# A planned attention kernel: first batch by head pairs, first weights ahead of later loads, second-batch masks by DMA

## The chip, the cores and the metric

The kernel runs on one core of a Trainium2 chip. The metric is device time in microseconds. Five instruction streams matter here, TensorE (PE in the profile), VectorE (DVE), ScalarE (ACT), GpSimd (POOL) and SyncE (SP), which issues most DMAs, and beside them the DMA queues. In the traces below each engine works through its own stream in order: an instruction that waits holds up what stands behind it on that engine.

The kernel before takes 283.2 us (median of 3, 282.56 to 283.69).

## The reference, cut to what matters

```python
# q, k, v: (4, 8, 768, 64) fp32; w_in: (512, 2048); w_out: (2048, 512)
gate = q @ mean_of_each_64_keys(k).T            # 12 key blocks; blocks after the query's own: -1e9
sel  = top3(gate) | {own block}                 # per query and head
attn = softmax(where(sel and causal, q @ k.T / 8, -1e9)) @ v
x    = attn.transpose(0, 2, 1, 3).reshape(3072, 512)
out  = gelu_tanh(x @ w_in) @ w_out              # (3072, 512) fp32
```

A batch is 768 rows and eight heads, which the kernel treats as four head pairs. Pairs 0 to 3 are batch 0, pairs 4 to 7 batch 1, and so on. For each batch the kernel runs attention, then the first linear layer with its gelu ("s1", 16 tiles of 1.30 us of TensorE), then the second ("s2").

## The kernel before

The kernel is a list of operations with estimated costs, dependencies and priorities. A planner inside the kernel, run while the kernel is built, walks a clock forward, picks an engine and a start time for every operation, and then emits all operations in the order of these planned starts. So the planner's estimates do not cost time themselves: they fix the order in which each engine must take its instructions. What an instruction really waits for at run time is its data, through semaphores.

```python
def load(p, key, at_least):                       # k, q or v of head pair p
    ...
    go = add({SP: 0.2}, emit_t if dve else emit,  # SyncE issues it: planned 0.2 us
             [free_sd.get((key, p - ...))], prio=10 * p)
    ld[key, p] = add({"DMA": 4.5 if dve else 2.0}, lambda _: None, [go, at_least],
                     prio=1000 * b + hp)          # planned: 4.5 us of DMA for a k or q from pair 5 on

def pre(p):                                       # preparation of one head pair
    ...                                           # k, q turned; block sums ks; ksb = masked sums
    for c in range(1, NC):                        # gate scores: five matmuls, 24 columns each
        nc.tensor.matmul(plan.buf["gt", p][:, (c - 1) * 24:c * 24],
                         T["qT32", p][:, c * 128:(c + 1) * 128], T["ksb", p]..., ...)
    ...                                           # top 3 of each row -> madd (DVE)
    if by_xbar(p):                                # pairs 8 to 15: mask turned by a DMA transpose
        go = add({SP: 0.1}, mask_dma, [sel], pr)
        m = add({"XBAR": 2.5}, lambda _: None, [go], pr)
    else:                                         # pairs 0 to 7: mask turned by TensorE
        m = add({PE: 0.27}, mask, [sel], pr, takes=("pre", ("mk", p)))
    mcs = [add({DVE: 0.4, ACT: 0.6}, mc(h), [m, ...], pr) for h in range(2)]   # mask copies

def heads(p):                                     # one head at a time: scores, exp, select, PV
    ...                                           # K = 76 rows: 64 of k/q and 12 of mask
```

SyncE issues the loads, by the trace, as k, q, v of pairs 0, 1 and 2, then k3 q3 k4 q4 v3 k5 q5; w_in starts at 29.6 us, beside q of pair 5, so the first loads of batch 1 go ahead of it. w_out is triggered from GpSimd when v3 and three attention outputs of batch 0 are planned to be there.

The softmax here doesn't subtract the row's maximum and nothing guards it: scores larger than these inputs give would overflow.

Of the kernel before, what the change touches and what calls it, by code (L numbers as in the profile page):

```python
# [33 lines left out]
class Plan:  # L34
# [17 lines left out]
    def solve(self):  # L52
        for n, op in enumerate(self.ops):
            op.n = n
            op.left = len(op.deps)
            op.ready = 0.0
            op.users = []
        for op in self.ops:
            for d in op.deps:
                d.users.append(op)  # L60
# [10 lines left out]
        while cand:  # L71
            best = None
            ests = []
            for op in cand:
# [13 lines left out]
                key=lambda x: (x[3].prio, x[3].n, x[1]))  # L88
# [32 lines left out]
def kernel(  # L121
# [22 lines left out]
    FIRST_DVE = 5  # L144
# [8 lines left out]
    atp = ctx.enter_context(tc.tile_pool(name="atp", bufs=7))  # L153
# [12 lines left out]
    bmask = const.tile([128, 2, NBLK], FP32)  # L166
# [5 lines left out]
    w_out16 = persist.tile([128, NF, DM], FP16)  # L172
    qT16, kT16, v16, madd = [], [], [], []
# [16 lines left out]
    def copy(eng, out, in_):  # L190
        if eng == ACT:
            nc.scalar.copy(out=out, in_=in_)
        else:
            nc.vector.tensor_copy(out=out, in_=in_)

    def by_dve(p):
        return p >= FIRST_DVE

    def by_xbar(p):
        return p >= 2 * HP  # L200
# [3 lines left out]
    ld = {}  # L204
    free_sd = {}

    def load(p, key, at_least):
# [11 lines left out]
        def emit_t(_):  # L219

            sd = io.tile([128, NC * 4, 32], FP32, tag=key, name=f"{key}_sd_{p}")
            for hh in range(2):
                for a in range(2):
# [5 lines left out]
        dve = key != "v" and by_dve(p)  # L229
        go = add({SP: 0.2}, emit_t if dve else emit,  # L230
                 [free_sd.get((key, p - (PV if key == "v" else PF)))],
                 prio=10 * p)
        ld[key, p] = add({"DMA": 4.5 if dve else 2.0}, lambda _: None, [go, at_least],
                         prio=1000 * b + hp)

    def cast_v(p, old):
        b, hp = divmod(p, HP)

        def emit(eng):
            copy(eng, v16[p % NB][:, :, :, 0:64], T["v", p])  # L240
        free_sd["v", p] = ld["v16", p] = add(
            {DVE: 0.47, ACT: 0.8}, emit, [ld["v", p], old],
            prio=1000 * (b - 1) + 599 + hp if b else 100 * hp - 55)

    def load_w(name, dst, src, n, deps, prio):
        res = []
        view = src.rearrange("(i p) f -> p i f", p=128)

        def emit(_):
            nc.gpsimd.dma_start(out=dst, in_=view)  # L250
        go = add({POOL: 1.3}, emit, deps, prio=prio)
        return add({"DMA": 12.0}, lambda _: None, [go], prio=prio)


    c_E = {}

    def consts():
        def e16(_):
            E32 = hd2.tile([128, S], FP32, tag="kT32", name="E32")
            T["E16"] = E16 = E32[0:12].bitcast(FP16)[:, 0:S]  # L260
            nc.gpsimd.memset(E16, MASKVAL)
            nc.gpsimd.affine_select(
                out=E16.rearrange("p (n w) -> p n w", w=64),
                in_=E16.rearrange("p (n w) -> p n w", w=64),
                compare_op=ALU.is_equal, fill=0.0,
                base=0, pattern=[[1, NBLK], [0, 64]], channel_multiplier=-1)
        c_E["E"] = add({POOL: 2.0}, e16, [], prio=-50)

        def gates(_):

            T["cgate"] = cgate = const.tile([128, NG, NBLK], FP32, name="cgate")
# [16 lines left out]

        def fill(i):
            def emit(_):  # L290
                for h in range(2):
                    nc.vector.tensor_copy(out=kT16[i][h][64:76, :],
                                          in_=T["E16"])
                    nc.vector.memset(qT16[i][h][64:76, 0:128], 0.0)
            c_E["fill", i] = add({DVE: 0.8}, emit, [c_E["E"]],
                                 prio=100 * i - 30)
# [4 lines left out]
            c_E["ones", i] = add({POOL: 0.5}, emit_p, [], prio=-40 + i)  # L301
# [7 lines left out]
    def pre(p):  # L309
        b, hp = divmod(p, HP)  # L310
        i = p % NB
        pr = 1000 * (b - 1) + 590 + hp if b else 100 * hp - 60
        slow = 1.0
        old = last.get(p - NB, {})

        def wk_t(a):
            def emit(_):
                w = plan.buf["wk", p, a]
                for c in range(3):
                    nc.tensor.transpose(  # L320
                        w[:, c * 128:(c + 1) * 128],
                        T["k", p][:, 3 * a + c].rearrange("p h d -> p (h d)"),
                        ident32)
            return emit

        def ks_r(a):
            def emit(_):
                if a == 0:
                    T["ks", p] = hd.tile([128, NBLK], FP32, tag="ks",
                                         name=f"ks_{p}")  # L330
                nc.vector.tensor_reduce(
                    out=T["ks", p][:, 6 * a:6 * a + 6],
                    in_=plan.buf["wk", p, a][:, 0:HALF].rearrange(
                        "p (n w) -> p n w", w=64),
                    op=ALU.add, axis=AXL.X)
            return emit

        def kc(a, h):
            def emit(eng):
                copy(eng, kT16[i][h][0:64, a * HALF:(a + 1) * HALF],  # L340
                     plan.buf["wk", p, a][64 * h:64 * h + 64, 0:HALF])
            return emit

        kcs, ksr, qcs = [], [], []
# [10 lines left out]
        if by_dve(p):  # L355
            t = add({DVE: 0.83}, tr("k"),
# [3 lines left out]
            def ks_all(_):  # L360
                T["ks", p] = hd.tile([128, NBLK], FP32, tag="ks",
                                     name=f"ks_{p}")
                nc.vector.tensor_reduce(
                    out=T["ks", p],
                    in_=T["kT32", p].rearrange("p (n w) -> p n w", w=64),
                    op=ALU.add, axis=AXL.X)
            ksr.append(add({DVE: 0.83}, ks_all, [t], pr))
# [6 lines left out]
            kcs = [add({DVE: 0.47, ACT: 0.7}, kc_all(h),  # L374
                       [t, old.get("k", None)], pr + 0.1) for h in range(2)]
        for a in range(0 if by_dve(p) else 2):
            t = add({PE: 0.33 * slow}, wk_t(a),
                    [ld["k", p], last.get(p - 3, {}).get("pre")], pr,
                    takes=("pre", ("wk", p, a)))
            if a == 1:  # L380
                free_sd["k", p] = t
            r = add({DVE: 0.47}, ks_r(a), [t] + ksr, pr)
            ksr.append(r)
            c0 = add({DVE: 0.47, ACT: 0.38}, kc(a, 0),
                     [t, old.get("k", None)], pr)
            c1 = add({DVE: 0.47, ACT: 0.38}, kc(a, 1),
                     [t, old.get("k", None)], pr)
            kcs += [c0, c1]
            add({"NONE": 0.0}, lambda _: None, [r, c0, c1], pr,
                gives=[("wk", p, a)])  # L390

        def ksb_m(_):
            T["ksb", p] = hd.tile([128, 2, NBLK], FP32, tag="ksb",
                                  name=f"ksb_{p}")
            nc.vector.tensor_tensor(
                out=T["ksb", p], in0=bmask,
                in1=T["ks", p].unsqueeze(1).to_broadcast([128, 2, NBLK]),
                op=ALU.mult)
        ksb = add({DVE: 0.1}, ksb_m, ksr, pr)
# [4 lines left out]
        def wq_t(a):  # L404
            def emit(_):
                w = plan.buf["wq", p, a]
                for c in range(3):
                    nc.tensor.transpose(
                        w[:, c * 128:(c + 1) * 128],
                        T["q", p][:, 3 * a + c].rearrange("p h d -> p (h d)"),  # L410
                        ident32)
            return emit

        def qc(a):
            def emit(eng):
                if a == 0:
                    T["qT32", p] = hd.tile([128, S], FP32, tag="qT32",
                                           name=f"qT32_{p}")
                copy(eng, T["qT32", p][:, a * HALF:(a + 1) * HALF],
                     plan.buf["wq", p, a][:, 0:HALF])  # L420
            return emit

        if by_dve(p):
            t = add({DVE: 0.83}, tr("q"),
# [3 lines left out]
        for a in range(0 if by_dve(p) else 2):  # L428
            t = add({PE: 0.33 * slow}, wq_t(a), [ld["q", p]], pr,
                    takes=("pre", ("wq", p, a)))  # L430
            if a == 1:
                free_sd["q", p] = t
            qcs.append(add({DVE: 0.47, ACT: 0.5}, qc(a),
                           [t] + qcs + [last.get(p - 3, {}).get("pre")], pr,
                           gives=[("wq", p, a)]))



        g = None
        for c in range(1, NC):  # L440
            def gate(_, c=c):
                nc.tensor.matmul(  # L442
                    plan.buf["gt", p][:, (c - 1) * 24:c * 24],
                    T["qT32", p][:, c * 128:(c + 1) * 128],
                    T["ksb", p].rearrange("p h n -> p (h n)"),
                    start=True, stop=True)
            g = add({PE: 0.1}, gate, [ksb, g] + qcs, pr,
                    takes=("pre", ("gt", p)), lag=0.2)

        def gm_e(_):  # L450
            T["gm", p] = hd.tile([128, NG, NBLK], FP32, tag="gm",
                                 name=f"gm_{p}")
            nc.vector.tensor_tensor(
                out=T["gm", p],
                in0=plan.buf["gt", p][:, 0:NG * NBLK].rearrange(
                    "p (g n) -> p g n", n=NBLK),
                in1=T["cgate"], op=ALU.add)
        gm = add({DVE: 0.2}, gm_e, [g, c_E["gates"]], pr, gives=[("gt", p)])

        def sel_e(_):  # L460
            mx8 = hd.tile([128, NG, 8], FP32, tag="mx8", name=f"mx8_{p}")
            for x in range(NG):
                nc.vector.max(out=mx8[:, x, :], in_=T["gm", p][:, x, :])
            sel = hd.tile([128, NG, NBLK], FP32, tag="sel", name=f"sel_{p}")
# [337 lines left out]
```

## Time and profile before

Lines of the page: the busy time of each engine; the span in 40 slices of 7.03 us, in tenths, for TensorE and for its granted clock; the shares of the chain that ended last.

```profile
PE 266.5 (95%) x2230; PEld 166.9 (59%) x2230; DVE 137.4 (49%) x438; ACT 189.4 (67%) x251; POOL 49.1 (17%) x119
...
PE   5998998799999999998999999999999999999994
...
PEclk9999999999999999999999999999999999999999
...
PE 76%; ACT 15%; DVE 3%; issue 3%; DMA 2%; POOL 1%; ACTq 0%; POOLq 0%; SPq 0%; DVEq 0%
```

TensorE is busy nearly everywhere, its granted clock is full in every slice, and the chain that ended last is 76% TensorE. But the first 50 us are only formally busy: 110 filler matmuls, whose results nobody reads, stand there. The chain of waits in order of time shows what really bounds the start (start us, length us, what):

```profile
49.38 0.93 ACT at_1_1_922 L571
50.37 0.43 POOL at_1_1_922 L585
50.85 0.39 PE bank_92 L597 x7
...
55.21 0.82 ACT gT_1010 L683
...
57.53 0.49 DVE qT_0_107 L194
58.04 0.68 ACT qT_1_108 L192
58.75 0.82 ACT gT_1010 L683
59.61 1.46 PE wide_88 L670 x8
```

Exponentials on ACT up to 51 us, then the first gelu at 55.21, then, after two waits of 0.5 us, s1 of batch 0 in steps of 1.30 us without a pause. (57.53 and 58.04 are the two copies of the mask of pair 4.)

| stage (us) | before |
|---|---|
| last exponential of batch 0 ends | 51.1 |
| first gelu of batch 0 | 55.2 |
| s1 of batches 0, 1, 2, 3 ends | 75.4, 140.6, 201.5, 256.8 |
| end of the span | 281.2 |

### The profile page before, as it was taken

What the parts mean: (1) busy time and instruction counts of PE and PEld (TensorE: products, weight loads), DVE (VectorE), ACT (ScalarE), POOL (GpSimd) and SP (SyncE); (2) the same over time, 40 slices, a digit from 0 to 9 for tenths busy, and PEclk for the clock granted to TensorE, in tenths of its full rate; (3) what the DMA queues carried; (4) which work ended last, traced back from release to release, by engine and by line L of the source; (5) the groups of instructions that cost most, each with busy time, mean ns of one, the idle gap of its engine ahead of it and who ended that gap; (6) DMA issues with size and microseconds to landing.
All of it is one profiled execution on the core that took longest, in us unless ns stands there. A gap on an engine that the chain in (4) does not pass through costs nothing.

```text
span 281.2 us, 5780 instructions
## 1 busy us (share of the span) xinstructions
PE 266.5 (95%) x2230; PEld 166.9 (59%) x2230; DVE 137.4 (49%) x438; ACT 189.4 (67%) x251; POOL 49.1 (17%) x119
## 2 busy tenths in 40 slices
PE   5998998799999999998999999999999999999994
PEld 4777775555657566564667565666566645565441
DVE  4587955770088787755578885594114310000000
ACT  2568998765889759476599992487799923664111
POOL 8012524100024213000024430000034400000000
PEclk9999999999999999999999999999999999999999
DMA  8999999999999987997667242230112231000212
GB/s 169 217 220 207 138 212 148 177 197 167 131 166 166 207 161 143 204 163 109 114 130 151 70 121 84 81 48 2 23 40 70 54 105 75 0 0 2 75 75 75
DMA packets 129211, 33.01 MB, mean 117 GB/s; under 512 B 123552, under 2 KB 125600, under 8 KB 129184
## 3 DMA queue, kind: packets, MB, share of 16 engines
q1 hardware_dynamic: 126592, 28.46, 54.2%
q0 software_dynamic: 2592, 4.19, 8.6%
q8 instruction: 17, 0.28, 0.4%
q14 instruction: 10, 0.08, 0.1%
HBM read 27.26 MB, written 6.29 MB: 119 GB/s over the span
## 4 chain that ended last, share of the span: by engine, by line
PE 76%; ACT 15%; DVE 3%; issue 3%; DMA 2%; POOL 1%; ACTq 0%; POOLq 0%; SPq 0%; DVEq 0%
PE wide_88 L670 13%; PE wide_89 L670 13%; PE bank_90 L700 9%; PE bank_93 L700 7%; PE bank_91 L700 6%; PE bank_92 L700 5%; PE wide_88 L559 4%; PE wide_89 L559 4%; DMA mT_1959<-madd_118 2%; PE bank_93 L597 1%; PE bank_92 L442 1%; PE bank_90 L734 1%; PE bank_91 L442 1%; PE bank_92 L597 1%; PE bank_91 L734 1%
## 5 line engine op out<-in xcount | busy, mean ns | idle before, releaser
L670 PEld LDWEIGHTS <-w_in_105 128*128 128x128 f16 x512 | 50.3, 103 | 32.3 <-issue 3.4
L700 PEld LDWEIGHTS <-gT_3361 128*128 128x128 f16 x96 | 9.4, 98 | 11.2
L734 PEld LDWEIGHTS <-ident_99 128*128 128x128 f16 x110 | 11.8, 115 | 5.6 <-DVE ident_99 L165 3.0
L700 PEld LDWEIGHTS <-gT_2670 128*128 128x128 f16 x96 | 9.0, 98 | 7.9
L670 PE MATMUL wide_89<-xT_1398,w_in_105 128*128 128x512 f16 x64 | 12.4, 325 | 1.4 <-ACT gT_1836 L683 1.4
L700 PEld LDWEIGHTS <-gT_1836 128*128 128x128 f16 x96 | 9.1, 99 | 7.7
L670 PE MATMUL wide_88<-xT_546,w_in_105 128*128 128x512 f16 x64 | 12.2, 325 | 1.1 <-ACT gT_1010 L683 1.1
L700 PEld LDWEIGHTS <-gT_1010 128*128 128x128 f16 x96 | 9.3, 104 | 6.1
L700 PE MATMUL bank_90<-w_out_106,gT_1836 128*128 128x512 f16 x48 | 12.7, 379 | 0.0
L670 PE MATMUL wide_88<-xT_2289,w_in_105 128*128 128x512 f16 x64 | 12.6, 325 | 0.0
L670 PE MATMUL wide_88<-xT_1398,w_in_105 128*128 128x512 f16 x64 | 12.6, 325 | 0.0
L670 PE MATMUL wide_89<-xT_2289,w_in_105 128*128 128x512 f16 x64 | 12.2, 325 | 0.0
L670 PE MATMUL wide_89<-xT_546,w_in_105 128*128 128x512 f16 x64 | 12.2, 326 | 0.0
L670 PE MATMUL wide_88<-xT_3039,w_in_105 128*128 128x512 f16 x64 | 12.0, 326 | 0.0
L670 PE MATMUL wide_89<-xT_3039,w_in_105 128*128 128x512 f16 x64 | 11.7, 326 | 0.0
L734 PE MATMUL bank_90<-ident_99 128*128 128x256 f16 x27 | 7.8, 303 | 3.5 <-DVE ident_99 L165 3.0
L530 ACT ACT_TABLE_LOAD x8 | 10.3, 1283 | 0.9 <-PEq L786 0.8
L734 PE MATMUL bank_92<-ident_99 128*128 128x256 f16 x38 | 9.8, 292 | 0.0
L700 PE MATMUL bank_93<-w_out_106,gT_1010 128*128 128x512 f16 x32 | 9.7, 379 | 0.0
L683 ACT ACTIVATE gT_1010<-wide_88 128x768 f16<-128x768 f32 x8 | 6.5, 809 | 4.2 <-PE wide_88 L670 4.2
L683 ACT ACTIVATE gT_2670<-wide_88 128x768 f16<-128x768 f32 x8 | 6.5, 807 | 4.2 <-PE wide_88 L670 4.2
L700 PE MATMUL bank_91<-w_out_106,gT_2670 128*128 128x512 f16 x32 | 9.2, 379 | 0.0
(917 smaller groups left out, 673.9 us busy)
## 6 DMA issues: line engine op xcount, KB each, us to landing
w_in_105<-in_moe_w_in_dram POOLq DMA_DIRECT2D x1, 2048.0 KB, 13.6
w_out_106<-in_moe_w_out_dram POOLq DMA_DIRECT2D x1, 2048.0 KB, 17.7
k_sd_136<-in_k_dram SPq DMA_DIRECT2D x2, 192.0 KB, 3.0
q_sd_143<-in_q_dram SPq DMA_DIRECT2D x2, 192.0 KB, 4.0
v_sd_148<-in_v_dram SPq DMA_DIRECT2D x2, 192.0 KB, 4.4
k_sd_153<-in_k_dram SPq DMA_DIRECT2D x2, 192.0 KB, 4.5
q_sd_158<-in_q_dram SPq DMA_DIRECT2D x2, 192.0 KB, 4.6
v_sd_163<-in_v_dram SPq DMA_DIRECT2D x2, 192.0 KB, 4.4
```

Of the source, the lines that this page charges most:

```text
L442: nc.tensor.matmul(plan.buf["gt", p][:, (c - 1) * 24:c * 24], T["qT32", p][:, c * 128:(c + 1) * 128], T["ksb", p].rearrange("p h n -> p (h ...
L530: nc.scalar.activation(out=t, in_=bmask[:, 0, 0:1], func=AF.Exp if key[0] == "exp" else AF.Gelu_apprx_tanh, bias=0.0, scale=1.0)
L559: nc.tensor.matmul(st[:, x:e], kT16[i][h][0:76, s0:s0 + 128], qT16[i][h][0:76, s0 + (x - cb):s0 + (e - cb)], start=True, stop=True)
L597: nc.tensor.matmul(pvv[:, qc, 0:65], at[:, cb + (qc - jc) * 128: cb + (qc - jc + 1) * 128], v16[i][:, jc, h, :], start=(gi == 0 and jc == ...
L670: nc.tensor.matmul(hps[:, u:e], w_in16[:, ci, f * 128:(f + 1) * 128], T["xT", b][:, ci, u:e], start=(ci == 0), stop=(ci == HP - 1))
L683: nc.scalar.activation(out=T["gT", b][:, f, :], in_=plan.buf["hps", b, f][:, 0:S], func=AF.Gelu_apprx_tanh, bias=0.0, scale=1.0)
L700: nc.tensor.matmul(plan.buf["ops", b, ti], T["gT", b][:, f, ti * 128:(ti + 1) * 128], w_out16[:, f, :], start=(f == 0), stop=(f == NF - 1))
L734: nc.tensor.matmul(plan.buf["warm", n][:, 0:256], ident16, z, start=True, stop=True)
```

## The change

The intent: shorten the start. Batch 0 is prepared by head pairs, its scores use the two row halves of the array for the two heads, one exponential covers both heads, and casts of v and q go to GpSimd. The first weights (w_in) no longer share the DMA engines with the loads of batch 1: these are held by a tiny DMA that reads w_in. The planner gets tighter DMA numbers. The masks of batch 1 are turned by DMA instead of TensorE, and gates use four column groups of the array at once.

The core of the diff (cut; the bodies of the new functions are left out, and two edits of the plan: the scores of a later batch are planned behind the s1 of the batch before, and output stores get a higher priority):

```diff
+            op.fifo = "DMA" in op.engines                  # planner: DMAs first come, first served
@@ load
-        go = add({SP: 0.2}, emit_t if dve else emit, [free_sd...], prio=10 * p)
-        ld[key, p] = add({"DMA": 4.5 if dve else 2.0}, ..., [go, at_least], ...)
+        go = add({SP: 2.0 if dve else 1.0}, emit_t if dve else emit, [free_sd..., held], ...)
+        ld[key, p] = add({"DMA": 2.5 if dve else 1.8}, ..., [go], ..., lag=1.6)
@@ w_in in two halves, 12 us of planned DMA for 2 MB as before
+    def hold(dep):
+        def emit(_):
+            x = const.tile([1, 16], FP16, name="held")
+            nc.sync.dma_start(out=x, in_=w_in16[0:1, 0, 0:16])
@@ pre: gate
+            for j in range(4):
+                nc.tensor.matmul(g[32 * j:32 * j + 32, 0:160]..., T["ksb", p]..., q5[:, j],
+                    start=True, stop=True, tile_position=(0, 32 * j))
@@ pre: mask; "first" is batch 0
-        if by_xbar(p):                      # pairs 8 to 15
-            go = add({SP: 0.1}, mask_dma, [sel], pr)
-            m = add({"XBAR": 2.5}, lambda _: None, [go], pr)
+        if first:
+            m = add({PE: 0.28}, mask, [sel], pr, takes=("pre", ("mk", p)))
+        else:                               # pairs 4 to 15
+            go = add({SP: 1.2}, mask_dma, [sel], -50)
+            m = add({"XBAR": 0.8}, lambda _: None, [go], pr, lag=1.7)
@@ batch 0
+    def heads2(p):                          # two heads at once, K = 64 on rows 0-63 and 64-127
+        ...
@@ order of loads
+    ... k0 q0 k1 q1 v0 k2 q2 v1 k3 q3 v2 v3
+    w_in (2 halves) after v2;  held = hold(w_ready["in", 0]);  loads of batch 1 behind held
+    w_out: [issued["q", HP + 1]]            # was [ld["v", 3], xts[0][2]]
```

## The prediction

> **What bounds the kernel now.** The page has PE busy 95% and the chain that ended last at 76% PE, 15% ACT. By stage (the chain in order of time, the timelines) there are two regimes.
>
> Start, 0 to 52 us: latency and ACT/DVE. The first exponential starts at 18.8 us, the last of batch 0 ends at 51.1, the first gelu is at 55.2, the first linear layer (s1) of batch 0 ends at 75.5 us. PE is only formally busy: 110 filler matmuls stand there. ACT spends some 20 us on 24 exponentials (0.81 us apart) and 15 on casts and copies (k halves 0.47, q 0.83, masks 0.68 us); DVE is as full (7.8 and 8.5 of 10 us in two windows).
>
> Afterwards PE: an f-tile of s1 takes 1.30 us, a row tile of the second layer (s2) 3.45, so 20.8 + 20.7 us a batch, plus about 9 of scores and 5 of PV. The s1 of batches 1, 2, 3 end at 140.5, 201 and 257 us: periods of 65, 60.5 and 56. The tail is 24 us. Only a shorter start or closed PE gaps count.
>
> **What the change does.**
> - Pair-wise preparation of batch 0: two 128-partition k copies instead of four of 64, one q cast and one mask copy instead of two; v casts and q casts (pairs 1-3) go to idle GpSimd; k block sums go from DVE (2 x 0.56 us a pair) to small PE matmuls. ACT loses 10-12 us of copies, DVE about 8.
> - Exponentials: same columns; 20 of 1024 (estimate from 0.81 us for 896: 0.92 us) and 4 of 256 (0.3): 19.6 us, unchanged.
> - Scores: K = 64 for each head on its half of the rows, plus a mask matmul. The Trainium skill, "TensorEngine Tiling (Array Packing)", Key Properties, says tiles can load and multiply in parallel, and that changing the mode drains the engine. If halves overlap, 2.24 us a pair (10,752 columns at 0.417 ns, halved), as before; if not, 4.5.
> - q1 lands before v0; no batch-1 loads before w_in. Before, w_in took 29.6 to 43.2 us; I expect issue near 25, landed by 39.
> - Batch 1 masks go by DMA transposes, gates become four column groups: under 0.4 us of PE a pair either way.
>
> **Critical path.** First exponential near 15.5 us; then ACT needs 19.6 + about 3 of copies plus gaps: last exponential at 40-42, first gelu 44-45, s1(0) ends near 65 (before 75.5). So 10-11 us saved. Part is given back: w_out (46.5 to 64.2 before) starts near 41, and w-loads starve small loads (one v load took 48.2 to 64.0). Pairs 5-7 then land at 58-74 us while wanted 10 us sooner, and each needs about 8 us of DVE and a mask transpose (2.6-4.6 us). I expect 2-4 us of PE stalls in batch 1, against 3-4 saved by tidier order there. Batches 2, 3 and the tail stay within 2 us. With some luck on gaps, net -14 us: 269 us; range 260 to 277. Faster by over 2%: 0.87; within 2%: 0.10; slower: 0.03.
>
> **What would show it.** Right: last batch-0 exponential near 41, ACT dense from 16 to 41; first gelu near 44.5; w_in landed by 39; period of batch 3 still 56; the K = 64 matmuls of two heads advance together. Wrong: exponentials waiting for PE (no overlap, drains) or for GpSimd casts; s1(0) waiting for w_in; batch-1 scores waiting for mask transposes or late k/q.
>
> **What would make it wrong.** Serial K = 64 matmuls (PE-bound start, gain halves); slow GpSimd casts blocking its in-order affine selects; batch 1 starved of loads; or a batch-1 period shorter than I think, giving 260.

## More of the kernel before

The preparation of pair 5 is worth two lines, the first of the VectorE timeline, the second of the TensorE timeline (start, busy, engine, line, operation; a wait before it would stand in brackets):

```profile
61.19 0.97 DVE L350 STREAM_TRANSPOSE qT_5_1170<-q_sd_382 128x768 f32<-128x768 f32 x1
```

```profile
75.22 0.30 PE L442 MATMUL bank_92<-ksb_1152,qT_5_1170 128*128 128x24 f32 x2
```

The q of pair 5 landed at 46.1 us and was used at 61.2, and the gate of pair 5 stands behind the whole s1 of batch 0. Nothing waits. The planner had believed that it lands at 63.3 us (its planned times can be printed while the kernel is built).

## The result, and the profile after

The changed kernel is correct and takes 302.2 us (median of 4, 300.46 to 302.78); before took 283.14 in the same rounds. Executions over 1.5% slower than the fastest of the same kernel are left out of the means. Ratios in this text are the mean time of one kernel's fast runs over that of the other's of the same rounds, so not quite the ratio of the medians quoted: 1.067, interval 1.063 to 1.071. It is slower, far outside the predicted range.

```profile
PE 271.5 (90%) x2278; PEld 158.9 (53%) x2278; DVE 127.2 (42%) x433; ACT 186.5 (62%) x241; POOL 56.1 (19%) x127
...
PE   7999999523699996996899999999999999999995
...
PEclk9999999959599997999799999999999999999999
...
GB/s 171 218 213 56 213 144 174 211 175 162 167 167 133 189 166 144 143 199 169 178 84 3 57 28 89 132 155 0 0 2 61 63 90 70 35 2 0 70 72 70
...
PE 72%; DMA 8%; DVE 8%; SPq 7%; ACT 2%; issue 2%; POOL 0%; DVEq 0%; ACTq 0%; POOLq 0%
```

The same lines as before, and the bytes moved in each slice (7.53 us now). TensorE is no longer full: slices 8, 9 and 10 (53 to 75 us) show 5, 2 and 3 tenths, and the granted clock falls to 5 tenths twice, right after. The chain now has 8% DMA, 8% VectorE and 7% SyncE's queue where it had 15% ACT. The fourth slice of the bytes (22.6 to 30.1 us, 56 GB/s) is the hold: the last loads of batch 0 land at 24.7, w_in is issued at 26.6, and the loads of batch 1 wait.

| stage (us) | before | after | difference of the stage |
|---|---|---|---|
| last exponential of batch 0 | 51.1 | 46.0 | |
| first gelu of batch 0 | 55.2 | 51.5 | -3.7 |
| s1 of batch 0 ends | 75.4 | 91.9 | +20.2 |
| s1 of batch 1 ends | 140.6 | 163.8 | +6.7 |
| s1 of batch 2 ends | 201.5 | 220.8 | -3.9 |
| s1 of batch 3 ends | 256.8 | 276.7 | +0.6 |
| end | 281.2 | 301.1 | 0.0 |

The differences add up to the 19.9 us between the spans. The start did get shorter, by 3.7 us to the first gelu. Most was lost in s1 of batch 0, which takes 40.4 us from its first gelu instead of 20.2. The TensorE timeline of that stretch (in brackets: idle time before, and what ended it):

```profile
52.42 4.06 PE L792 MATMUL wide<-xT,w_in 128*128 128x512 f16 x24
56.32 0.71 PE L857 MATMUL bank<-ident 128*128 128x256 f16 x5
65.67 0.76 PE L449 MATMUL bank<-qT,ksb 128*32 128x160 f32 x8 [8.64 <-DVE ksb L412]
66.37 3.77 PE L792 MATMUL wide<-xT,w_in 128*128 128x512 f16 x16
69.97 0.60 PE L857 MATMUL bank<-ident 128*128 128x256 f16 x4
78.12 13.79 PE L792 MATMUL wide<-xT,w_in 128*128 128x512 f16 x72 [7.55 <-ACT gT L805]
```

There are two pauses. In front of the second group of s1 matmuls stands a gate of batch 1, of pair 5, and it waits 8.64 us. Then s1 waits 7.55 us for a gelu. The VectorE timeline tells why the gate was late, and the ACT timeline why the gelu was:

```profile
58.69 0.98 DVE L372 STREAM_TRANSPOSE kT<-k_sd 128x768 f32<-128x768 f32 x1 [5.40 <-DMA k_sd<-in_k_dram]
...
64.56 0.98 DVE L372 STREAM_TRANSPOSE qT<-q_sd 128x768 f32<-128x768 f32 x1 [3.91 <-DMA q_sd<-in_q_dram]
...
76.52 0.32 DVE L206 COPY qT<-mT 12x640 f16<-12x640 f16 x1 [7.74 <-DMA mT<-madd]
84.68 0.65 DVE L206 COPY qT<-mT 12x640 f16<-12x640 f16 x2 [7.85 <-DMA mT<-madd]
```
```profile
76.52 0.72 ACT L202 COPY qT<-mT 12x640 f16<-12x640 f16 x1 [9.40 <-DMA mT<-madd]
77.26 1.51 ACT L805 ACTIVATE gT<-wide 128x768 f16<-128x768 f32 x2
```

The gate waits for q of pair 5, which landed at 64.3 us. The planner had believed 47.7 and had therefore put this gate among the s1 tiles. The gelu waits behind a copy of the mask of pair 4, and that waits for a DMA transpose. The selection of pair 4 was done on VectorE at 53.3 us; the transpose takes 3.4 us. It landed 23.2 us later. SyncE's timeline shows where it stood:

```profile
53.06 7.21 SPq L231 DMA_DIRECT2D q_sd<-in_q_dram  x2
...
73.14 1.31 SPq L510 DMA_TRANSPOSE mT<-madd  x1
74.58 2.39 SPq L231 DMA_DIRECT2D q_sd<-in_q_dram  x4
```

The mask was issued at 73.14, behind the issues of loads for pairs 5 to 7; the mask of pair 5 followed at 81.20. While w_out moves (46.4 to 62.3 us), SyncE takes 7.21 us to issue two pieces of a load; the four of the load at 74.58 take 0.6 us each.

The pauses have a second cost. A table of windows from the same trace gives a granted clock of 0.70 from 66 to 70 us and 0.85 from 78 to 92. Sixteen s1 matmuls took 3.77 us there and 72 took 13.79; at 1.30 us for eight they take 2.6 and 11.7. So the clock took about 3.2 us more. The Trainium skill, "TensorE: Matmul & The Clock Gate", Part 1, says that an idle window of about 3.4 us brings the array to half clock and that some 3.4 us of work bring it back; the trace agrees in kind (pauses of 8.64 and 7.55 us, then 0.70 and 0.85 on average over windows).

The 6.7 us of batch 1 are of the same kind. Two pauses stand there, and the chain leads both back to a copy that waited for a mask by DMA (the masks landed at 114.2 and 141.9):

```profile
115.95 0.69 PE L723 MATMUL wide<-qT,kT 76*128 76x512 f16 x2 [2.43 <-ACT at L736]
...
144.27 3.08 PE L792 MATMUL wide<-xT,w_in 128*128 128x512 f16 x10 [4.08 <-ACT gT L805]
```

### The profile page after: what moved, and what is told of

Same layout as the page of the kernel before. It is cut to its first block, busy times and chain, and to the rows that moved or that the text cites. A ratio compares the mean times of both kernels' runs of the same rounds, so it can differ in the third digit from the quotient of the medians.

```text
span 301.1 us, 5868 instructions
## 1 busy us (share of the span) xinstructions
PE 271.5 (90%) x2278; PEld 158.9 (53%) x2278; DVE 127.2 (42%) x433; ACT 186.5 (62%) x241; POOL 56.1 (19%) x127
## 4 chain that ended last, share of the span: by engine, by line
PE 72%; DMA 8%; DVE 8%; SPq 7%; ACT 2%; issue 2%; POOL 0%; DVEq 0%; ACTq 0%; POOLq 0%
PE wide L792 26%; PE bank L823 22%; SPq L231 7%; PE wide L723 7%; DMA mT<-madd 5%; PE bank L762 4%; PE bank L857 4%; DMA q_sd<-in_q_dram 3%; PE wide L583 3%; PE bank L349 2%; PE bank L355 2%; PE bank L449 2%; DVE kT L372 1%; DVE mx L476 1%; PE bank L636 1%
## 5 line engine op out<-in xcount | busy, mean ns | idle before, releaser
L792 PE MATMUL wide<-xT,w_in 128*128 128x512 f16 (+1 forms) x512 | 90.2, 336 | 11.6 <-ACT gT L805 11.6
L823 PE MATMUL bank<-w_out,gT 128*128 128x512 f16 x384 | 98.4, 380 | 0.5 <-DVE gx L462 0.5
L792 PEld LDWEIGHTS <-w_in 128*128 128x128 f16 x512 | 51.0, 100 | 49.0 <-issue 17.0
L805 ACT ACTIVATE gT<-wide 128x768 f16<-128x768 f32 x64 | 51.4, 809 | 29.2 <-PE wide L792 29.0
L736 ACT ACTIVATE at<-wide 128x896 f16<-128x896 f32 x72 | 60.8, 914 | 2.9 <-POOL at L750 1.5
L750 POOL TENSOR_SCALAR_AFFINE_SELECT at<-at 128x256 f16<-128x256 f16 x72 | 31.1, 432 | 165.1 <-ACT at L736 164.9
L823 PEld LDWEIGHTS <-gT 128*128 128x128 f16 x384 | 35.7, 97 | 35.5 <-issue 1.8
L723 PE MATMUL wide<-qT,kT 76*128 76x512 f16 (+1 forms) x192 | 39.9, 310 | 2.4 <-ACT at L736 2.4
L202 ACT COPY osb<-bank 128x512 f32<-128x512 f32 x18 | 10.5, 583 | 33.7 <-PE bank L823 30.1
L762 PEld LDWEIGHTS <-at 128*128 128x128 f16 x504 | 24.4, 98 | 11.4 <-POOL at L750 3.0
L762 PE MATMUL bank<-v,at 128*128 128x65 f16 x504 | 27.6, 195 | 0.2 <-POOL at L750 0.2
L857 PEld LDWEIGHTS <-ident 128*128 128x128 f16 x110 | 11.4, 111 | 5.8 <-DVE ident L166 1.8
```

The source lines that it names most:

```text
L202: nc.scalar.copy(out=out, in_=in_)
L723: nc.tensor.matmul(st[:, x:e], kT16[i][h][0:76, s0:s0 + 128], qT16[i][h][0:76, s0 + (x - cb):s0 + (e - cb)], start=True, stop=True)
L736: nc.scalar.activation(out=T["at", u][:, 0:n], in_=plan.buf[("st",) + u][:, 0:n], func=AF.Exp, bias=0.0, scale=SCALE)
L750: nc.gpsimd.affine_select(out=dg, in_=dg, compare_op=ALU.is_ge, fill=0.0, base=0, pattern=[[0, 2], [1, 128]], channel_multiplier=-1)
L762: nc.tensor.matmul(pvv[:, qc, 0:65], at[:, cb + (qc - jc) * 128: cb + (qc - jc + 1) * 128], v16[i][:, jc, h, :], start=(gi == 0 and jc == ...
L792: nc.tensor.matmul(hps[:, u:e], w_in16[:, ci, f * 128:(f + 1) * 128], T["xT", b][:, ci, u:e], start=(ci == 0), stop=(ci == HP - 1))
```

## The experiments

All edits are to the changed kernel unless it is said otherwise, they are shown cut to the lines that matter, and all kernels gave correct results. Where the expectations use letters for theories: A is that the late loads are the cause (held, or slowed by w_out), B that the masks by DMA are, C that the changed work itself is, and D that it is the order of instructions, fixed against load times that the chip doesn't keep. Before had medians of 283.05 (e1 to e4), 282.06 (e5 to e8), 282.87 (e9 to e12), 283.34 (e13 to e16) and 282.86 (e17, e18). Ratios are to these; the column of medians holds all runs (e10 and e18 have one slow run, e13 two). Within 2% of before are e11, e13, e14, e16, e17 and e18; e15 is unclear; all others are slower.

| run | us | ratio to before | 95% interval |
|---|---|---|---|
| the change | 302.2 | 1.067 | 1.063 to 1.071 |
| e1_nohold | 319.7 | 1.131 | 1.127 to 1.135 |
| e2_maskpe | 298.2 | 1.055 | 1.051 to 1.058 |
| e3_woutlate | 307.0 | 1.087 | 1.081 to 1.092 |
| e4_gatelate | 299.8 | 1.061 | 1.057 to 1.064 |
| e5_nohold2 | 313.5 | 1.111 | 1.106 to 1.115 |
| e6_woutwait | 307.4 | 1.090 | 1.087 to 1.093 |
| e7_before_hold | 289.6 | 1.028 | 1.022 to 1.034 |
| e8_nohold2_maskpe | 308.2 | 1.092 | 1.089 to 1.095 |
| e9_slack | 310.6 | 1.097 | 1.091 to 1.104 |
| e10_calibsp | 290.8 | 1.026 | 1.021 to 1.032 |
| e11_calibsp_maskpe | 285.9 | 1.010 | 1.004 to 1.016 |
| e12_actq | 303.4 | 1.072 | 1.069 to 1.075 |
| e13_startonly | 288.6 | 1.004 | 0.994 to 1.014 |
| e14_calibsp2_maskpe | 284.8 | 1.002 | 0.995 to 1.010 |
| e15_startonly_hold | 287.8 | 1.015 | 1.007 to 1.022 |
| e16_calibsp2_maskpe_nopool | 284.9 | 1.005 | 0.997 to 1.012 |
| e17_hold_otpe | 279.2 | 0.987 | 0.985 to 0.989 |
| e18_calib_otpe | 286.0 | 1.008 | 1.005 to 1.012 |

### First: is one part to blame? (e1 to e4)

**e1_nohold**, the loads of batch 1 not held:

```diff
-    held = hold(w_ready["in", 0])
+    held = None
```

> The changed kernel with one part undone: the loads of batch 1 no longer wait for w_in. Theory A (late loads: k and q of pair 5 land at 64 us because w_out starves them, and the gate of pair 5 has a fixed place inside the first linear layer of batch 0): they land near 32 us, that layer runs from about 50 to 72 us without a pause, total about 284 us. Theory B (mask transposes by DMA stuck in the SP queue behind loads): only the 9 us pause of PE at the gate goes, the second one of 8 us stays, about 293. Theory C (the pair-wise start itself, GpSimd casts or the lower clock): still above 298.

Measured: 319.7 us, 17 us more than the change. The run has a flaw: the new plan moved the w_out trigger up to 25 us, in the middle of batch 0, so the exponentials of batch 0 ended only at 62.3. It is not a clean removal of the hold; e5 repeats it with the trigger kept.

**e2_maskpe**, the masks of batch 1 back on TensorE:

```diff
-        if first:
+        if first or p < 2 * HP:
             m = add({PE: 0.28}, mask, [sel], pr, takes=("pre", ("mk", p)))
```

> The changed kernel with the masks of batch 1 transposed on PE again. Theory A: only the second pause (ACT waits for the mask of pair 4, PE idle 70 to 78 us) goes, the first (57 to 66 us, gate of pair 5) stays: 290 to 295 us. Theory B: nearly all of the loss goes: 283 to 287. Theory C: above 298.

Measured: 298.2 us, 4 us better. s1 of batch 0 ends at 82.6 instead of 91.9; its pauses are 2.7 and 5.5 us, the longer one still at the gate of pair 5. The mask wait is a real part of the loss, but batch 1 gave back more than half of the gain, with pauses of 5.4, 1.6 and 2.7 us.

**e3_woutlate**, w_out triggered after the q load of pair 7, so that the loads of pair 5 have the DMA for themselves:

```diff
-        if p == HP + 1:
-            w_ready["out"] = load_w(..., [issued["q", HP + 1]], 30)
+        if p == 2 * HP - 1:
+            w_ready["out"] = load_w(..., [ld["q", 2 * HP - 1]], 30)
```

> The changed kernel with w_out issued only when k and q of pair 7 have landed. Theory A: k and q of pair 5 land before 50 us, both pauses in the first linear layer of batch 0 go, it ends near 72 us instead of 92; some is given back since the second layer of batch 0 now waits for w_out (landing near 75 us): total 283 to 290. Theory B: the second pause stays, 291 to 295. Theory C: above 298.

Measured: 307.0 us, and the experiment missed its aim. A dependency in the plan sets only the order, and GpSimd had nothing to wait for in front of the trigger: w_out still started at 45.6 us, while s2 of batch 0, moved back in the plan, began only at 118.9. Nothing follows for w_out. What it did teach is that a planned dependency is no wait at run time.

**e4_gatelate**, the gates of pairs 5 to 7 placed behind s1 of batch 0:

```diff
+        late = [s1_mm[0][-1]] if HP < p < 2 * HP else []
-        g = add({PE: 0.45}, gate, [ksb] + qcs, ...)
+        g = add({PE: 0.45}, gate, [ksb] + qcs + late, ...)
```

> The changed kernel with the gates of pairs 5 to 7 placed after the first linear layer of batch 0 on PE; the DMA order is left alone. Theory A says that the late landing hurts only through the fixed place of that gate: the first pause (9 us) goes, the layer ends by 84 us, but the data of pair 5 are as late as before, so the attention of batch 1 gets part of it back: 292 to 300 us. Theory B: the second pause decides, under 2 us of gain. Theory C: no change.

Measured: 299.8 us. The 8.64 us pause at the gate is gone (5.0 us of waiting for a gelu stand in its place) and s1 of batch 0 ends at 82.5, 9.4 us sooner; but now a score matmul of batch 1 waits 7.5 us for a mask copy at 92.4. Only 2.4 us remain of it: moving one waiting instruction lets the next one behind it wait.

### Second: the hold and w_out, cleanly (e5 to e8)

**e5_nohold2**: as e1, and w_out kept behind the last exponential of batch 0 (`[issued["q", HP + 1], exps[0][-1]]`).

> The hold undone as in e1, but w_out kept where the changed kernel has it in GpSimd's order (behind the last selects of batch 0), since in e1 it slipped to 25 us and starved all. Theory A2 (the hold lets the small loads stand still from 25 to 36 us and makes every later load 6 to 10 us later): q of pair 5 lands before 47 us, no pause at the gates in the first linear layer of batch 0, which ends near 72 us; total 284 to 290. Theory B (masks by DMA behind loads in the SP queue): a pause for a mask of 5 us or more stays, total 291 to 296.

Measured: 313.5 us, although q of pair 5 now lands at 47.6, 17 us sooner than with the hold. But the plan moved too: without the hold it believes 32.7 us for this load, so that against its own plan the load is still 15 us late. The VectorE timeline:

```profile
80.41 0.32 DVE L206 COPY qT<-mT 12x640 f16<-12x640 f16 x1 [26.66 <-DMA mT<-madd]
```

The selection of pair 4 was ready at 47.9 us, its transpose was issued at 76.8 and landed at 80.4. With more loads in front of it in SyncE's queue the mask stood even longer, and VectorE with it. Theory A in its plain form falls: without the hold the loads land sooner and the kernel is slower. Their lateness against the plan was not removed, so theory D is not tested here.

**e6_woutwait**, the aim of e3 with a real wait: GpSimd copies one column of q of pair 7 before it triggers w_out.

```diff
+            def seen(_):
+                x = const.tile([128, 1], FP32, name="seen")
+                nc.gpsimd.tensor_copy(out=x, in_=T["q", 2 * HP - 1][:, 0, 0:1])
+            gate_w = add({POOL: 0.1}, seen, [ld["q", 2 * HP - 1]], 30)
-                                    [issued["q", HP + 1]], 30)
+                                    [gate_w], 30)
```

> The changed kernel with a real wait: GpSimd reads a piece of q of pair 7 before it starts w_out (e3 had changed only the planner's order, and w_out still started at 45.6 us). Theory A3 (w_out itself starves k and q of pair 5): they land by 54 us instead of 64, the first pause shrinks to under 2 us, the first linear layer of batch 0 ends before 82 us; but the second layer of batch 0 waits for w_out (landing near 78 us): total 290 to 299. If w_out does not matter, no change of the first pause and 302.

Measured: 307.4 us. This time the aim was met: w_out starts at 71.0 and q of pair 5 lands at 54.2, 10 us sooner than in the change. The pauses in s1 of batch 0 are 7.7 and 9.6 us all the same, and both are now gelus behind mask copies. The mask of pair 4 landed at 66.8; that of pair 5 was issued at 71.9, beside w_out, and took until 83.3. So early data for pair 5 doesn't cure it either, as long as masks stand in that queue.

**e7_before_hold**: the kernel before, with the same hold on its batch-1 loads (a tiny DMA that reads w_in in front of them on SyncE).

> The kernel before with one part of the change alone: loads of batch 1 wait until w_in has landed. Theory A2: q of pair 5 lands 15 us later or more, a pause appears in or after the first linear layer of batch 0, total 291 to 300 us (3 to 6% slower than before). Theory B (the hold is harmless, the mask route costs): within 3 us of before.

Measured: 289.6 us, 1.028 of before. The hold costs the kernel before 7.5 us by itself (medians), and the profile shows it in batch 1, whose s1 waits 4.45 us for a DMA transpose of an attention output, not in batch 0.

**e8_nohold2_maskpe**: e5 and e2 together.

> e5 and e2 together: no hold, w_out kept, batch-1 masks on PE. If hold and mask route are the whole loss, what is left is the shorter start: first linear layer of batch 0 ends near 70 us (before 75.5) and the total is 276 to 282 us, below before. If something else in the change costs, it stays above 286.

Measured: 308.2 us. The start is better (s1 of batch 0 ends at 88.2), but at 109 us VectorE waits 14.24 us for the mask of pair 8, the first that still goes by DMA (selection done at 91.3, issued at 106.0). The same wait, one batch later. And in s1 of batch 0 the gate of pair 5 still waits 7.5 us for its q, which this plan, as that of e5, expects at 32.7 us. So neither the hold, nor w_out, nor the mask of batch 1 is the cause by itself.

### Third: the planner's numbers (e9 to e12)

What is left is the order itself. The planner of the change believes in 2.5 us of DMA and 2.0 of SyncE for a k or q load; in the trace the four pieces of one take about 2.8 us of DMA and 2.3 to 3.2 of SyncE, and the 2 MB of w_out take 16 us where it believes 12. The planner of before believed in 4.5 us: too much, so the data of batch 1 was early.

The kernels were built again and their plans printed. They show the point directly, the place that the plan gives to the gate of pair 5:

| kernel | q of pair 5 planned | landed | gate of pair 5 planned | s1 of batch 0 ends, planned |
|---|---|---|---|---|
| before | 63.3 | 46.1 | 64.4 | 64.4 |
| the change | 47.7 | 64.3 | 50.9 | 66.0 |
| e10 | 72.0 | 67.6 | 74.7 | 68.8 |
| e11 | 72.0 | 67.0 | 75.4 | 69.0 |
| e17 | 68.3 | 65.1 | 69.5 | 64.9 |

Of these five, only the change has the gate inside s1. The length of the whole plan warns of nothing: 258 us for before, 259 for the change, 261 for e17.

**e9_slack**: the DMA numbers of before alone, nothing for SyncE.

```diff
-        ld[key, p] = add({"DMA": 2.5 if dve else 1.8},
+        ld[key, p] = add({"DMA": 4.5 if dve else 2.0},
```

> The changed kernel with one number of its planner put back: a k or q load from batch 1 on is planned at 4.5 us of DMA time as before, not 2.5 (and a v load at 2.0, not 1.8). The same instructions in another order. Theory D (the orders of PE, DVE, ACT and SP are fixed against loads that are planned earlier than they land: q of pair 5 planned for 47.7 us, landed at 64.3; in the kernel before planned for 63.3, landed at 46.1): the plan is now later (q of pairs 5, 6, 7 at 58, 81, 92 us, landing at about 64, 72, 80), the pauses shrink to under 6 us together, total 284 to 293. If the changed work itself is the cause: above 298.

Measured: 310.6 us, worse than the change. VectorE waits longer for the same mask:

```profile
83.64 0.65 DVE L206 COPY qT<-mT 12x640 f16<-12x640 f16 x2 [15.44 <-DMA mT<-madd]
```

It was selected at 58.7 and issued at 80.7, 22 us in SyncE's queue. With longer DMA times and the same SyncE times the planner thought the queue of issues empty when it was not. The first form of theory D, "the DMA number is what is wrong", falls.

**e10_calibsp**: the numbers that the trace of the change shows, for DMA, SyncE and weights together.

```diff
-        go = add({SP: 2.0 if dve else 1.0}, ...
+        go = add({SP: 2.9 if dve else 1.9}, ...
-        ld[key, p] = add({"DMA": 2.5 if dve else 1.8},
+        ld[key, p] = add({"DMA": 2.9 if dve else 1.95},
-        return add({"DMA": 12.0 * n / 8192}, ...
+        return add({"DMA": 16.0 * n / 8192}, ...
-                                    [issued["q", HP + 1]], 30)
+                                    [issued["q", HP], exps[0][-1]], 30)
```

> The changed kernel with its planner given the measured DMA: 2.9 us for a k or q load, 1.95 for v, the same times for SP to issue them (SP is held up by the queue), 16 us for each weight matrix, and w_out taken to start at the end of batch 0 ahead of pair 5, as it does. Theory D: no pause over 3 us in the first linear layer of batch 0, which ends by 76 us; total 277 to 288. If the changed work itself is the cause: above 298.

Measured: 290.8 us (median of all; the three fast runs lie between 289.5 and 292.0, and the profiled run was the slow one). That is 3 us over the expected range, but 11 us of the 19 are back with no instruction of the kernel changed, only their order. The largest pause in s1 of batch 0 is 1.46 us, then 108 matmuls run without one, to 77.9:

```profile
58.88 19.02 PE L792 MATMUL wide<-xT,w_in 128*128 128x512 f16 x108
```

**e11_calibsp_maskpe**: e10 and e2 together.

> e10 with the masks of batch 1 transposed on PE. Theory D alone: within 3 us of e10. Theory B (the place of the mask transposes in the SP queue has a cost of its own that no plan removes): 5 us or more below e10; total 273 to 284, perhaps below before.

Measured: 285.9 us, ratio 1.010. 16 of the 19 us are back. The step from e10, 4.9 us, lies between what was expected of theory D alone (3) and of a cost of the mask's own (5 or more); the intervals of the two ratios don't overlap, so some such cost is there. After its first matmul TensorE is idle 7.6 us, as in before (8.0), although q of pair 5 lands at 67.0, 2.7 us later than in the change.

**e12_actq**: the change, with its DMA transposes issued by ACT instead of SyncE, so that they don't stand behind loads.

```diff
-            nc.sync.dma_start_transpose(
+            nc.scalar.dma_start_transpose(
```

> The changed kernel with all transposes by DMA issued from ACT instead of SP, so that none stands behind loads; loads and plan otherwise as they are. Theory B: a mask lands within 5 us of its selection (for pair 4 the changed kernel took 23 us), the second pause goes, DVE does not wait for masks over 4 us: total 288 to 295, the first pause of 9 us left. If the SP queue is not what delays the masks: 300 or more.

Measured: 303.4 us. No mask stands in a queue now: that of pair 4 was selected at 52.30 and issued at 52.34, that of pair 5 took 4.3 us in all (69.5 to 73.8) instead of 15.9. But the one of pair 4 moved beside w_out and took 9.8 us to land, not the expected 5. s1 of batch 0 ends 8 us sooner, at 83.8, but the gate of pair 5 still waits 10.4 us for its q, and later ACT stands up to 6.84 us for output stores, which are now the ones behind loads on SyncE. The queue in front of the mask is shown to be SyncE's; moving the mask out of it is not enough.

### Fourth: is any of it the changed arithmetic? (e13 to e16)

**e13_startonly**: all changed arithmetic of batch 0, with these parts of before: no hold, SyncE 0.2, DMA 4.5 and 2.0, no first-come rule, w_in after q3, w_out after three attention outputs, and the masks of batch 1 on TensorE. The order among the loads of batch 0 stays that of the change.

> The changed start of batch 0 (head pairs, row halves, column-group gates, GpSimd casts) with the load order and the planner's DMA numbers of before, no hold, batch-1 masks on TensorE. If the loss is load order and fixed instruction orders alone: first gelu of batch 0 at 50 to 53 us, no TensorE pause over 4 us in its first linear layer, time 272 to 282 us, faster than before. If the changed arithmetic itself costs: 286 us or more, with the loss in stages that wait for no load and no mask.

Measured: four runs from 283.9 to 291.7, two of them counted as slow; the two fast ones give 1.004 (0.994 to 1.014). It reached neither the expected gain nor a loss. The profiled run, a slow one, has a pause that isn't the clock's, on GpSimd and on TensorE:

```profile
42.23 0.83 POOL L204 CAST v<-v_sd 128x768 f16<-128x768 f32 x1 [8.66 <-DMA v_sd<-in_v_dram]
```
```profile
43.47 0.40 PE L643 MATMUL bank<-v,at 128*128 128x65 f16 x4 [6.50 <-POOL at L630]
```

Without the hold, k and q of pair 4 were issued ahead of v of pair 3, which then moved beside w_in and landed at 42.1 us. Its cast on GpSimd waited, and behind it in the same queue waited a select of batch 0 whose data had long been there. The casts on GpSimd and the order of loads belong together.

**e14_calibsp2_maskpe**: e11 with the SyncE number of batch 0 back at 1.0.

> e11 with the planner's SyncE estimate of batch 0 back at 1.0 us. If e11's remaining loss is its slipped start (last exponential of batch 0 at 49.8 instead of 46): last exponential near 46 and 280 to 284 us. If the slipped start was hidden behind later data: 285 to 290 us and a TensorE pause of 3 us or more inside the first linear layer of batch 0.

Measured: 284.8 us, 1.002. The last exponential still ends at 49.1. After it a new detail shows: GpSimd takes the w_out trigger (49.51, 1.17 us) before the last select (50.69).

**e15_startonly_hold**: e13 with the hold back, the only difference.

> e13 with the hold put back, the only difference. If the hold is a cost of its own: k and q of pairs 4 and 5 land about 10 us later than in e13 and the time is 5 to 10 us over e13 (the hold cost 6.5 us on the kernel before). If the hold only matters together with the optimistic planner numbers: within 2 us of e13.

Measured: 287.8 us, 1.015 (1.007 to 1.022). The intervals of e13 and e15 overlap, so the cost of the hold here stays open; it is not the 5 to 10 us that I expected. Its profile is the interesting thing: v of pair 3 lands at 24.8, s1 of batch 0 runs without a pause and ends at 73.6, 1.8 us before that of before. What it loses, it loses in batch 1:

```profile
123.24 1.44 PE L799 MATMUL wide<-xT,w_in 128*128 128x512 f16 x4 [7.89 <-DMA xT<-xn]
```

That is a DMA transpose of an attention output, which was ready at 115.0 and stood in SyncE's queue until 119.5, as the masks did.

**e16_calibsp2_maskpe_nopool**: e14 with the casts of v and q off GpSimd.

```diff
-            {DVE: 0.47, ACT: 0.8} if b else {POOL: 1.0}, emit,
+            {DVE: 0.47, ACT: 0.8}, emit,
-            q16s = [add({POOL: 1.0} if p else {ACT: 0.8}, q16, ...
+            q16s = [add({DVE: 0.56, ACT: 0.8}, q16, ...
```

> e14 with the v and q casts of batch 0 back on VectorE and ScalarE. If the GpSimd casts are harmless and free ACT and DVE as intended: last exponential of batch 0 later by 1 to 3 us and time 1 to 4 us over e14. If they slow VectorE or block GpSimd's own work: faster than e14 by 1 to 4 us.

Measured: 284.9 us, the same as e14. With this order the casts on GpSimd neither gain nor cost anything that can be measured (the intervals are 1.5% wide).

### Last: the rest of the in-order places (e17, e18)

**e17_hold_otpe**: e15, with the attention outputs of batch 1 turned by TensorE as well, and w_out triggered after the last select of batch 0.

```diff
-        if p >= HP + 2:          # attention outputs turned by DMA
+        if p >= 2 * HP:
-                                    [ld["v", 3], xts[0][2]], 400)
+                                    [ld["v", 3], xts[0][3]], 400)
```

> e15 with the attention outputs of batch 1 transposed by TensorE instead of DMA, and the w_out load triggered after the last select of batch 0 instead of in front of it. If the DMA transposes in the SyncE queue are what is left: no TensorE pause over 3 us in the first linear layer of batch 1 (7.9 in e15), time 276 to 281 us, below before. If the pause was cover for work that has to be done anyway: 284 us or more.

Measured: 279.2 us (279.07 to 279.46), 0.987 of before (clear of noise, but a gain under 2%), and against the change, dividing the two ratios, 0.925. It beats both kernels. TensorE is 97% busy and the chain has 83% of it:

```profile
PE 268.2 (97%) x2310; PEld 158.5 (57%) x2310; DVE 132.5 (48%) x434; ACT 187.3 (68%) x242; POOL 55.3 (20%) x127
...
PE 83%; ACT 6%; DMA 3%; DVE 3%; issue 2%; SPq 1%; POOL 0%; ACTq 0%; DVEq 0%; POOLq 0%
```

The lines that decide are these, TensorE first, then VectorE:

```profile
60.06 13.16 PE L799 MATMUL wide<-xT,w_in 128*128 128x512 f16 x80 [0.17 <-ACT gT L812]
...
77.81 0.48 PE L449 MATMUL bank<-qT,ksb 128*32 128x160 f32 x8
```
```profile
65.35 0.98 DVE L372 STREAM_TRANSPOSE qT<-q_sd 128x768 f32<-128x768 f32 x1 [4.67 <-DMA q_sd<-in_q_dram]
77.55 0.69 DVE L206 COPY osb<-bank 128x512 f32<-128x512 f32 x1 [11.23 <-ACT at L743]
```

This kernel has the same hold, and w_out moves from 48.4 to 64.7. Its q of pair 5 lands at 65.1 us, 0.8 us later than in the change. VectorE even waits 4.67 us for it, and later 11.23 us for an output tile, at no cost. The planner believed 68.3, so nothing of s1 stands behind this load: the gate of pair 5 is at 77.81, and s1 runs 80 matmuls without a pause while the load is still on its way. The lateness of the data is the same; its cost is a pause of 8.64 us at the gate in one order and none in the other. (The other pause of the change, 7.55 us, was for a mask by DMA, and here TensorE turns that mask.)

**e18_calib_otpe**: e16 with the same two edits.

> e16 with the same two edits. If they are worth their pauses (2.5 and 3.5 us, and 1.2 us at the start): first gelu of batch 0 near 53.5 instead of 54.7, time 277 to 281 us. If not: 284 us or more.

Measured: 286.0 us, no gain. The first gelu is at 53.1, sooner than in e16 (54.7), and s1 of batch 0 ends at 73.7, but s1 of batch 1 waits 4.7 us for a gelu at 122 and ends at 146.9. Its own plan was 4 us longer than that of e17 (265 and 261), but plan lengths have not told the times apart. Why this set of numbers does worse in batch 1 has not been looked into.

## Why the prediction was wrong

**The step that failed** is: "I expect 2-4 us of PE stalls in batch 1, against 3-4 saved by tidier order there." The mechanism was named just before it (w_out starves small loads, "pairs 5-7 then land at 58-74 us while wanted 10 us sooner", "a mask transpose (2.6-4.6 us)"), and the landing times were nearly right: q of pair 5 at 64.3, of pair 6 at 71.6, of pair 7 at 79.9. What failed is the place and the size. I reckoned that late preparation of batch 1 would delay batch 1. In an in-order machine it delays whatever stands behind it, and the planner, believing 47.7 us for q of pair 5, had put its gate and the mask copies among the tiles of s1 of batch 0. The plan wanted that q 16.6 us before it landed, not 10. The two pauses measured 8.64 and 7.55 us, with some 3.2 us of lower clock, in place of 2 to 4. Another 6.7 us went in batch 1, again for masks, where 3 to 4 had been counted as saved.

**The mask transpose** was costed as the DMA alone. The DMA took 3.4 us, within the 2.6 to 4.6 of before, but from selection to landing it was 23.2 us for pair 4 and 15.9 for pair 5, nearly all of it in SyncE's queue. The Trainium skill, "DMA: Bandwidth & Descriptors", under "Issuing engines are not separate DMA queues", says that issuing from several engines saves only sequencer time, "which is usually small relative to the DMA itself". Here the measurement decides otherwise: beside w_out the issue of one 96 KB piece held SyncE for up to 4.60 us, where one takes about 0.5 us otherwise, and the mask stood 19.8 us behind such issues for a transfer of 3.4. (In e12, with ACT issuing, the masks of pairs 4 and 5 did not stand at all, and took 9.9 us beside w_out and 4.3 without it.)

**The start gained less than half.** Predicted: first exponential at 15.5, last at 40 to 42, first gelu at 44 to 45. Measured: 18.2, 46.0 and 51.5. ScalarE's work was sized right: between the first and the last exponential it is busy 23.3 us (19.6 and 3 predicted). TensorE was not. The k of pair 0 has landed at 4.6 us, but TensorE takes 42 fillers first; the plan lets them end at 4.5 us, and they ended at 9.1:

```profile
1.84 7.26 PE L857 MATMUL bank<-ident 128*128 128x256 f16 x42 [1.84 <-DVE ident L166]
8.93 0.82 PE L349 MATMUL bank<-ident,k_sd 128*128 128x128 f32 x6
```

That is the same fault in small, and before has it too (k landed at 4.8, first transpose at 7.9). The block sums of k on TensorE then take 1.25 us for each of the four pairs (12 fp32 matmuls, 112 ns apart), which I had called small, and from there on the exponentials wait six times, 3.6 us in all, for scores: a sign that the prediction had named. After the last exponential come two normalisations, ScalarE's copy and the transpose, 5.5 us where before needed 4.1; that both heads of a pair now end together is a likely reason, not a tested one. So the 10 to 11 us of saving were worth 3.7 at the first gelu, and e17, whose s1 of batches 0 and 1 has no pause, is 1.3% faster than before, not 5%. What the start would gain with fewer fillers was not run.

**What was right.** The row halves overlap: two K = 64 matmuls of two heads start 3 ns apart and the next pair follows after 213 ns for 512 columns, with about 100 ns more where the mode changes (308 ns to the next matmul of 128 rows). The Trainium skill, "TensorEngine Tiling (Array Packing)", Key Properties, says that tiles work in parallel and that a mode switch drains the array; the trace agrees, and gives the drain its size. The column groups cost little (four matmuls start 7 ns apart, 0.41 us of TensorE for a gate). A 1024-column exponential costs about 0.92 us. The casts on GpSimd took 0.82 us and were not slow. w_in landed at 41.3 (39 predicted), the tail is unchanged, and the period of batch 3 is 55.9 (56 predicted); batch 2 took 3.9 us less than before, where at most 2 had been said.

**What the cause is, and how far it is shown.** The loss is in the order of instructions, fixed in advance against DMA and SyncE times that the chip doesn't keep. For 11 of the 19 us it is shown by e10, where only planned numbers and the w_out trigger changed and the pause at the gate went. e11 brings 16 us back, with q of pair 5 later than in the change; its 5 us more are a matter of the mask's route. e17 brings 23 us back with the changed arithmetic of batch 0, the same hold and the same late q of pair 5, but it also takes the masks and the attention outputs of batch 1 off SyncE, so that its gain is not the order's alone. e6 shows that early loads don't help while the masks stand in SyncE's queue, and e9 that correcting the DMA number without the SyncE number makes it worse. What no run isolates: which of the planner edits in e15 and e17 (the DMA number, the SyncE number, the first-come rule, the places of the w_in and w_out triggers) carries how much, how order and route share the gain of e17, and what the hold costs in the good order.

## What to carry to other kernels

Where an order is fixed in advance, an estimate of a load's arrival is not a guess about time but a decision about what will stand behind that load: in these runs an estimate on the late side cost no wait (before was 17.2 us on that side), and one on the early side stopped the engine with the critical work (16.6 us on that side, a pause of 8.64). Print the plan and see what stands behind a late load before you predict. When you make such a plan tighter, correct the DMA time, the issue time and the length of the issuing queue together, from a trace, and see that no instruction of a later stage stands in front of the present one unless its data has already landed. Small transfers that somebody waits for (masks, transposes) should not share an in-order issuing engine with bulk loads; here TensorE turned one in 0.44 us, five matmuls by the trace of e17.

The Trainium skill, "Perfetto Trace Analysis", Optimization Strategy, advises to find the gaps on the engine of interest and the semaphore that blocks it. Here that named the gate of pair 5 and the mask copy at once. It is only half of the way: e4 took the first gap away and had 2.4 us of 8.64 for it, since the next instruction in line waited in its place.

## What the Trainium skill lacked or had wrong

- "DMA: Bandwidth & Descriptors", "Issuing engines are not separate DMA queues": the cost of issuing is called usually small relative to the DMA. On SyncE two issues of 96 KB took 7.21 us while a 2 MB load was moving, and a ready transpose of 3.4 us waited 19.8 us for its turn. The page doesn't speak of the issuing engine being held back in this way.
- The same page, "Queues, rings and completion order", describes round-robin arbitration between queue rows but gives no figure for a small load beside a large one. In the change a 96 KB piece took 3.7 to 3.8 us from issue to landing in the median; beside w_out it took up to 14.4 us there and 16.0 in before (48.9 to 64.8); a mask transpose issued beside w_out took 11.4 us instead of 3.4 (71.9 to 83.3 in e6).
- The same page, "DMA Transpose (X-bar)", lists constraints but no time for a small transpose from issue to landing: a mask of 640 columns took 2.6 to 4.0 us in the change, 9.8 beside w_out in e12.
- "TensorEngine Tiling (Array Packing)", Key Properties: a mode switch drains the array; no size is given. Here about 100 ns.
- "TensorE: Matmul & The Clock Gate", Part 1, names an idle window of about 3.4 us before the clock is halved. In the change a pause of 2.43 us (113.5 to 115.9) was followed by a mean granted clock of 0.57 from 116 to 120 us, so a shorter one can be enough.
